# RetNet retention and SwiGLU: float32 Strassen products replaced by three 12-bit products each

## The chip, the cores and the metric

The kernel runs on one core of one Trainium2 chip. TensorE (PE in the profile) multiplies matrices into PSUM, whose eight banks hold 128 x 512 float32 values each; VectorE (DVE), ScalarE (ACT) and GpSimd (POOL) work element by element, GpSimd on SBUF alone; DMA queues move data between HBM and SBUF, and most are issued from SyncE (SP). The metric is the device time in microseconds of one execution; the median of three runs of the kernel before is 708.61 us (707.46 to 709.76).

## The reference

Retention over 4 sequences of 768 tokens with 8 heads of 64, and then a SwiGLU block on the 3072 tokens:

```python
for t in range(S):
    state = gamma[None, :, None, None] * state + np.einsum('bhd,bhe->bhde', k[:, :, t], v[:, :, t])
    y[:, :, t] = scale * np.einsum('bhd,bhde->bhe', q[:, :, t], state)
...
x = np.ascontiguousarray(attn_out.transpose(0, 2, 1, 3)).reshape(B * S, H * D)
g = x @ w_gate
silu = g * (1.0 / (1.0 + np.exp(-g)))
val = x @ w_val
return (silu * val @ w_out).astype(np.float32)
```

d_model is 512 and d_ff is 1536. q, k, v and the result are float32; the three weights come as 64-bit floats, and the kernel makes float32 of them from their two words.

## The kernel before

**Segments and stages.** Tokens are taken in four segments of 768: three chunks of 128 positions in each of two sequences. x^T lies in SBUF as `xT`, the hidden activations as `hT` (12 blocks of 128 of d_ff, each with the tokens of both sequences). For each segment there is an up stage (gate and value products, silu, multiply) and a down stage (the product with w_out), and beside the down stage of segment s runs the retention of segment s + 1, whose small matmuls are put between the big ones (`retention`, from L497, all through `mm` at L502). So the kernel goes: start, up 0, down 0 with retention 1, up 1, down 1 with retention 2, and so on to down 3.

**Up stage of segment 0** (`up`, L673): for each of 12 blocks f, one level of Strassen in Winograd's form. Two sequences by two halves of d_model meet gate and value by two halves of d_model, seven products instead of eight, each of two float32 matmuls of 384 columns (L679). Their sums lie in `ring` (weights) and `xs` (activations). Meanwhile the weights come in from HBM as 64-bit words, are turned into float32 on ScalarE, VectorE and GpSimd (`convert_a`, `convert_b`, `convert_c`), summed on VectorE (`sums_t`, L284) and written back to HBM for later segments (`keep_wt`). The string table `beside` says what goes beside which product.

**Up stages of segments 1 to 3** (`up2`, L749): a second level of Strassen. 21 units of seven products each (seven at the upper level for each of three groups of four blocks), each product two float32 matmuls of 192 columns (L790). Results are put together from PSUM by VectorE and ScalarE, and by additions of whole tiles on GpSimd (`stage`; its calls show up at L755 and L825). Units are loaded into a ring of six, and their sums are made once (`sums_u`, L159) and saved.

**Down stages** (`down`, L866): one level of Strassen over both sequences, both halves of d_ff and both halves of the output; for each of three chunks u seven products of six float32 matmuls of 256 columns (L873, L883). w_out is held in SBUF with its sums (`wot`, 12 x 7 x 256 floats per partition between six tiles), and four sums of hidden activations are made for each chunk (`sum_h`, L861).

**Order.** The schedule is written by hand. In `up2` each operation is an event at a time in units of matmuls, and the events are sorted; in `down`, `step` counts products and `DUE` says at which count a part of the retention is put in. An engine works through its instructions in the order in which they were issued, with semaphores for what it needs from others. SP's DMAs are likewise in order.

Of the kernel before, what the change touches and what calls it, by code (L numbers as in the profile page):

```python
# [10 lines left out]
F32 = mybir.dt.float32  # L11
I32 = mybir.dt.int32
# [4 lines left out]
P = 128  # L17
# [14 lines left out]
NQ = NF // 4  # L32
NU = 7 * NQ
RING = 6
# [4 lines left out]
NTAB = GDEC0 + NP  # L39


@with_exitstack
def tile_retnet_swiglu(
# [13 lines left out]

# [9 lines left out]
    def place(name, n):  # L90
        return consts.tile([P, n], F32, name=name)

    hsp, midp, loadp, iop = (place(nm, n) for nm, n in (
        ("hsp", 4 * FH * P), ("midp", 6 * TA), ("loadp", 8 * 512), ("iop", 6 * 512)))
    hT = consts.tile([P, NF, 2, TH], F32, name="hT")
    ring = [consts.tile([P, 7 * KH * P], F32, name=f"ring{i}") for i in range(RING)]
    banks = [psum.tile([P, 512], F32, name=f"bank{i}") for i in range(8)]
    turn = {}

    def bank(tag):  # L100


        own = {"s": (4, 5), "y": (6, 7)}[tag]
        turn[tag] = turn.get(tag, -1) + 1
        return banks[own[turn[tag] % len(own)]]


    chunks = {}

    def load_chunk(c, places):  # L110

        for t in places:
            own = chunks.setdefault(c, [])
            nc.sync.dma_start(out=t, in_=(k_t, q_t, v_n, k_n)[len(own)][c])
            own.append(t)

    def seg_chunks(s):

        p, pos = divmod(s * L, NCK)
        return [(2 * p + i) * NCK + pos + j for j in range(L) for i in range(2)]  # L120

    tab = consts.tile([P, NTAB], F32, name="tab")


    wt = {}
    wot = [consts.tile([P, 7, DH], F32, name=f"wot{j}") for j in range(FH)]
    T3, B22, B12, T1, B11, B21, T2, T4 = 0, 1, 2, 2, 3, 4, 5, 6


    U1, U11, U21, U3, U22, U2, U4 = range(7)  # L130
    unit_b = [kept.tile([P, 7, 2, 4, P], F32, name=f"unitb{q}", tag=f"unitb{q}")
              for q in range(NQ)]
    unit_t = [kept.tile([P, 2, 7, P], F32, name=f"unitt{n}", tag=f"unitt{n}")
              for n in range(NU)]
    PRODUCTS = (1, 5, 6, 2, 7, 3, 4)
    SLOT = {1: B11, 5: T1, 6: T2, 2: B21, 7: T3, 3: B22, 4: T4}
# [4 lines left out]
    def keep_wt(f):  # L141

        q, b, h = f // 4, f // 2 % 2, f % 2
        nc.sync.dma_start(out=unit_b[q][:, :, h, ds(2 * b, 2)],
                          in_=wt[f].rearrange("p a (k f) -> p a k f", k=KH))

    units = {}

    def load_unit(n, whole, slot=None):
        t = ring[n % RING if slot is None else slot]  # L150
        t = t.rearrange("p (h a b) -> p h a b", h=2, a=7)
        if whole:
            nc.sync.dma_start(out=t, in_=unit_t[n])
        else:
            nc.sync.dma_start(out=t[:, :, ds(U11, 4)],
                              in_=unit_b[n // 7][:, SLOT[PRODUCTS[n % 7]]])
        units[n] = t

    def sums_u(n, engine=nc.vector):  # L159

        w = units[n]
        sub = engine.tensor_tensor

        def first():
            sub(w[:, :, U1 : U3 + 1 : 3], w[:, :, ds(U3, 2)], w[:, :, U11 : U3 + 1 : 2],
                op=ALU.subtract)

        def last():
            sub(w[:, :, U4], w[:, :, U21], w[:, :, U2], op=ALU.subtract)  # L169
            nc.sync.dma_start(out=unit_t[n], in_=w)  # L170

        return [first,
                lambda: sub(w[:, :, U2], w[:, :, U22], w[:, :, U1], op=ALU.subtract),
                last]


# [3 lines left out]
    def span(piece):  # L180

        kind, a, h = piece
        if kind == "up":
            return wt[a], B22, 4
        return wot[a], (B22, B11)[h], 2

    def load_piece(piece):

        kind, a, h = piece
# [5 lines left out]
        else:  # L195
            top, low = (w_out[ts(a + FH * i, P)] for i in range(2))
            parts = ([(low[:, DH:], 0), (top[:, DH:], 1)],
                     [(top[:, :DH], 0), (low[:, :DH], 1)])[h]
        to, slot, n = span(piece)
        to = to[:, ds(slot, n)]  # L200
        if w_gate.dtype != F32:
# [4 lines left out]
        for src, i in parts:  # L206
            if w_gate.dtype != F32:
                src = src.bitcast(U32)
            if len(src.shape) == 3:
                c = src.shape[1]  # L210
                t = to[:, i:].rearrange("p a b -> p (a b)")[:, : c * src.shape[2]]
                t = t.rearrange("p (c f) -> p c f", c=c)
            else:
                t = to[:, i]
            nc.sync.dma_start(out=t, in_=src)

# [40 lines left out]

    def convert_c(piece, halves=1):
        if piece in raw:
            d, lo, hi = words_of(piece)
            n = d.shape[1] // halves
            for i in reversed(range(halves)):
                nc.gpsimd.tensor_tensor(d[:, ts(i, n)].bitcast(I32),
                                        d[:, ts(i, n)].bitcast(I32),  # L270
                                        lo[:, ts(i, n)].bitcast(I32), op=ALU.add)
            del raw[piece]

    def sums_t(piece, parts=range(3)):
        kind, a, h = piece
        w = span(piece)[0]
        sub = nc.vector.tensor_tensor
# [3 lines left out]
        for o, x, y in [((both, w[:, ds(B22, 2)], w[:, ds(B12, 2)])),  # L281
                          ((w[:, T2], w[:, B22], w[:, T1])),
                          ((w[:, T4], w[:, B21], w[:, T2]))][parts[0] : parts[-1] + 1]:
            sub(o, x, y, op=ALU.subtract)  # L284
        if kind == "up" and parts[-1] == 2:
            keep_wt(a)

    pieces = [("up", f, 0) for f in range(NF)] + [
        ("down", n % FH, 1 - n // FH) for n in range(2 * FH)]
    sign_banks = {0: (0, 1), 1: (4, 5)}

    def scale(what, engine):
        return lambda n: what(cs[n], engine)
# [35 lines left out]
    beside[11, 4] = "k4 k5"  # L334
    beside[8, 2] = "D D"

    def aside(f, place):
        if (f, place) == (8, 2):
            raw_places["down"][:0] = [hsp[:, ts(i, 1024)] for i in range(2)]
        do(beside.get((f, place), ""))  # L340

    to_load = {"up": [("up", f, 0) for f in range(NF)],
               "down": [("down", n % FH, 1 - n // FH) for n in range(2 * FH)]}
# [105 lines left out]

# [698 lines left out]
```

## Time and profile before

The profiled execution has a span of 706.6 us, 2.0 us below the median of the runs. The stages, from the chain of waits and the profile's windows (busy times in us):

| stage | from-to, us | length | TensorE | VectorE | ScalarE | GpSimd |
|---|---|---|---|---|---|---|
| start | 0-29.5 | 29.5 | 24.3 | 16.5 | 13.1 | 7.5 |
| up 0, first part | 29.5-69.1 | 39.6 | 36.8 | 32.5 | 28.6 | 12.1 |
| up 0, rest | 69.1-143.6 | 74.5 | 74.5 | 64.1 | 52.8 | 32.6 |
| down 0 + retention 1 | 143.6-216.5 | 72.9 | 71.3 | 56.5 | 16.1 | 13.0 |
| up 1 | 216.5-317.6 | 101.1 | 98.6 | 83.4 | 34.3 | 53.3 |
| down 1 + retention 2 | 317.6-386.7 | 69.1 | 69.1 | 36.5 | 16.6 | 11.9 |
| up 2 | 386.7-483.4 | 96.7 | 96.7 | 62.0 | 34.3 | 48.5 |
| down 2 + retention 3 | 483.4-552.6 | 69.2 | 69.1 | 35.1 | 16.1 | 12.8 |
| up 3 | 552.6-649.4 | 96.8 | 96.8 | 62.2 | 34.3 | 48.5 |
| down 3 | 649.4-701.7 | 52.3 | 52.2 | 17.3 | 5.0 | 0.0 |
| last copies and stores | 701.7-706.6 | 4.9 | 1.6 | 0.0 | 0.5 | 0.0 |

Busy time of TensorE is that of records whose ends are modelled and which overlap, so it says that there are few gaps, not how much of the array works. The page's first part gives the shares over the whole span and the number of instructions:

```profile
PE 691.0 (98%) x5132; PEld 601.3 (85%) x5132; DVE 466.0 (66%) x830; ACT 251.5 (36%) x514; POOL 240.2 (34%) x147
```

### The profile page before, as it was taken

How to read it: one execution, taken by the hardware profiler on the slowest of the kernel's cores; microseconds unless marked ns; L12 is line 12 of the kernel's file. 1: busy time of each engine (PE TensorE's matmuls, PEld its weight loads, DVE VectorE, ACT ScalarE, POOL GpSimd, SP SyncE). 2: the span in 40 equal slices, each digit the busy share in tenths (PEclk: the TensorE clock that was granted, in tenths of full speed). 3: DMA queues.
4: the chain of work that ended last, by engine and by line, in shares of the span. 5: the costliest groups of instructions: out<-in, count | busy, mean ns of one | idle time of the engine just before them, and what ended most of it. 6: DMA issues, size and time to landing. Idle time of an engine off the chain costs nothing.

```text
span 706.6 us, 12979 instructions
## 1 busy us (share of the span) xinstructions
PE 691.0 (98%) x5132; PEld 601.3 (85%) x5132; DVE 466.0 (66%) x830; ACT 251.5 (36%) x514; POOL 240.2 (34%) x147
## 2 busy tenths in 40 slices
PE   7998999999999899999999999999999999999998
PEld 7654555578888899998888999998888999999887
DVE  3887998778858987876353675657551666657420
ACT  2658777511333233421322333331222324342000
POOL 0334444403300738280230455474210182644000
PEclk9999999999999999999999999999999999999999
DMA  9798897657999858581570555562291255630010
GB/s 316 261 369 281 284 300 239 176 138 221 354 355 369 316 183 306 206 252 45 188 305 1 186 198 198 194 210 67 84 374 38 86 205 209 209 105 0 24 37 30
DMA packets 63356, 139.92 MB, mean 198 GB/s; under 512 B 6336, under 2 KB 30272, under 8 KB 63296
## 3 DMA queue, kind: packets, MB, share of 16 engines
q1 hardware_dynamic: 59552, 132.81, 55.6%
q10 hardware_dynamic: 3744, 6.29, 2.4%
q8 instruction: 40, 0.66, 0.4%
q14 instruction: 20, 0.16, 0.1%
HBM read 102.51 MB, written 36.57 MB: 197 GB/s over the span
## 4 chain that ended last, share of the span: by engine, by line
PE 83%; DMA 8%; DVE 3%; issue 3%; ACT 2%; POOL 1%; SPq 0%; DVEq 0%; ACTq 0%; POOLq 0%
PE bank L790 38%; PE bank L873 23%; PE bank L679 13%; PE bank L502 4%; PE bank L883 4%; DMA out_dram<-iop 1%; DMA unitt<-ring 1%; DMA loadp<-in_w_gate_dram 1%; DMA hsp<-in_w_gate_dram 1%; DMA hT<-in_v_n_dram 1%; DMA loadp<-in_q_t_dram 1%; DMA ring<-unitb 1%; DMA hT<-in_k_t_dram 1%; DVE ring L169 0%; DVE iop L755 0%
## 5 line engine op out<-in xcount | busy, mean ns | idle before, releaser
L790 PE MATMUL bank<-loadp,ring 128*128 128x192 f32 x720 | 140.6, 327 | 0.7 <-DVE iop L755 0.7
L873 PE MATMUL bank<-wot,hsp 128*128 128x256 f32 x576 | 129.4, 382 | 0.0
L790 PEld LDWEIGHTS bank<-loadp,ring 128*128 128x128 f32 x720 | 120.4, 190 | 2.4 <-DVE iop L755 1.3
L873 PEld LDWEIGHTS bank<-wot,hsp 128*128 128x128 f32 x576 | 108.1, 190 | 16.0 <-issue 1.4
L755 DVE TENSOR_TENSOR iop<-bank,iop 128x384 f32<-128x384 f32 x144 | 79.7, 556 | 50.1 <-PE bank L790 46.8
L790 PE MATMUL bank<-xs,ring 128*128 128x192 f32 x432 | 88.0, 326 | 1.2 <-DVE iop L755 1.2
L755 ACT COPY hsp<-bank 128x384 f32<-128x384 f32 x90 | 42.9, 478 | 102.5 <-PE bank L790 94.0
L825 POOL TENSOR_TENSOR hT<-iop 128x768 f32<-128x768 f32 x36 | 67.1, 1863 | 35.4 <-DVE iop L755 35.4
L755 POOL TENSOR_TENSOR iop<-hsp,midp 128x768 f32<-128x768 f32 x9 | 16.3, 1812 | 174.8 <-ACT hsp L755 140.3
L790 PEld LDWEIGHTS bank<-xs,ring 128*128 128x128 f32 x432 | 73.1, 190 | 1.5 <-DVE iop L755 1.5
L790 PE MATMUL bank<-xT,ring 128*128 128x192 f32 x324 | 66.3, 327 | 0.2 <-DVE midp L755 0.2
L873 PE MATMUL bank<-wot,hT 128*128 128x256 f32 (+1 forms) x300 | 65.9, 373 | 0.5 <-ACT iop L960 0.4
L679 PE MATMUL bank<-xs,ring 128*128 128x384 f32 x192 | 64.7, 488 | 1.1 <-ACT iop L700 0.5
L873 PEld LDWEIGHTS bank<-wot,hT 128*128 128x128 f32 x300 | 54.9, 190 | 8.4 <-DVE iop L948 0.6
L679 PEld LDWEIGHTS bank<-xs,ring 128*128 128x128 f32 x192 | 36.1, 190 | 27.8 <-ACT iop L700 1.1
L790 PE MATMUL bank<-hsp,ring 128*128 128x192 f32 x288 | 56.7, 326 | 0.5 <-ACT hsp L755 0.5
L790 PEld LDWEIGHTS bank<-xT,ring 128*128 128x128 f32 x324 | 54.7, 190 | 1.4 <-DVE iop L755 0.8
L755 DVE TENSOR_TENSOR midp<-bank,midp 128x384 f32<-128x384 f32 x72 | 39.9, 554 | 17.9 <-PE bank L790 14.8
L679 PE MATMUL bank<-xT,ring 128*128 128x384 f32 x144 | 49.8, 489 | 1.8 <-DVE hT L716 1.6
L790 PEld LDWEIGHTS bank<-hsp,ring 128*128 128x128 f32 x288 | 48.4, 190 | 0.8 <-ACT hsp L755 0.8
L944 DVE TENSOR_TENSOR iop<-bank,iop 128x256 f32<-128x256 f32 x12 | 5.1, 424 | 64.7 <-PE bank L873 51.8
L679 PEld LDWEIGHTS bank<-xT,ring 128*128 128x128 f32 x144 | 26.9, 190 | 21.9 <-DVE hT L716 2.2
(152 smaller groups left out, 973.4 us busy)
## 6 DMA issues: line engine op xcount, KB each, us to landing
ring<-unitt SPq DMA_DIRECT2D x50, 896.0 KB, 4.6
unitt<-ring SPq DMA_DIRECT2D x21, 896.0 KB, 6.0
unitb<-ring SPq DMA_DIRECT2D x12, 896.0 KB, 7.0
ring<-unitb SPq DMA_DIRECT2D x21, 512.0 KB, 5.9
out_dram<-iop ACTq DMA_DIRECT2D x23, 256.0 KB, 2.5
loadp<-in_w_val_dram SPq DMA_DIRECT2D x18, 256.0 KB, 4.1
loadp<-in_w_gate_dram SPq DMA_DIRECT2D x9, 512.0 KB, 6.6
midp<-in_w_out_dram SPq DMA_DIRECT2D x12, 256.0 KB, 6.0
```

What stands on the lines that cost most here:

```text
L502: nc.tensor.matmul(o, a, b, start=start, stop=True, skip_group_check=True)
L679: nc.tensor.matmul(o, w[:, slot, k], a[:, k], start=(start and k == 0), stop=(stop and k == KH - 1), skip_group_check=True)
L755: events.append((t, len(events), lambda: fn(*args, **kw)))
L790: nc.tensor.matmul(o[:, h], w[:, h, slot], rhs, start=(start and h == 0), stop=True, skip_group_check=True)
L825: by_block(9.5, 13.5, lambda r: pool(to[:, r], u2[:, r], p5[:, r], op=add))
L873: nc.tensor.matmul(o[:, cols], a[:, k], wot[k][:, slot, cols], start=(start and k == 0), stop=(k == FH - 1), skip_group_check=True)
L883: nc.tensor.matmul(o, a_dn(0, 0, u)[:, k], wot[k][:, B11], start=(k == 0), stop=(k == FH - 1), skip_group_check=True)
L944: tt(ev[0][:, DH:], wb, u2, op=ALU.add)
```

## The change

Up 0 stays as it was. In the rest, four things change.

**Three 12-bit products.** A float32 operand is split into a high part of 12 bits and a rest, in tiles of type float32r (`R12`) with three planes, such that the three plane-wise products, added up in one PSUM bank, make the product up to a factor. The one operand is split by `near_*` (plane 0 on ScalarE, plane 1 on VectorE from two SBUF tiles, plane 2 on GpSimd as their sum), the other by `far_*` (plane 0 on ScalarE, plane 1 on GpSimd, plane 2 on VectorE from two SBUF tiles, and a scaling of it on ScalarE). Each float32 matmul becomes three float32r matmuls.

**Up stages 1 to 3** (`up3`): one level of Strassen instead of two. For each block f there are seven products of three planes by two halves, of 384 columns; the weights, with their sums, are loaded from HBM as in up 0's order (`w_up`) and split anew in every segment, in groups of 768, 768 and 256 columns (`weights`). The activations' seven operands are split once for a segment, in the down stage before it (`make_x`).

**Down stages:** no Strassen. For each block f and each of six groups of 128 tokens, three matmuls of 512 columns into one of banks 0 to 5, which gather all 12 blocks. The hidden activations of a block are split just ahead (`h_split`); w_out is no longer held but streamed: in down 0 read as float32 and split, with the planes written to HBM (`w_dn3`), in later ones read as planes.

**Retention** uses banks 6 and 7 alone: scores, mixing in two parts with a small read between them (`fence`), and states take turns in them, each at its own half step (`PARTS`).

Everything after the start is an event with a planned time; all events are sorted by it. The planned times set only the order on each engine.

```diff
+CUT = 1.0 + 2.0 ** -13
+FAR = 4096.0
+ONE = 4095.0
...
+    def near_a(o, x):
+        act(o[0], x, AF.Copy, scale=CUT / FAR)
+
+    def near_b(o, x):
+        stt(o[1], f32(o[0]), -FAR, x, op0=mul, op1=add)
+
+    def near_c(o):
+        pool(o[2], f32(o[0]), f32(o[1]), op=add)
+
+    def far_a(o, x):
+        act(o[0], x, AF.Copy, scale=CUT)
+
+    def far_b(o, x):
+        pool(o[1], f32(o[0]), x, op=sub)
+
+    def far_c(o):
+        stt(o[2], f32(o[0]), 1.0 / FAR, f32(o[1]), op0=mul, op1=sub)
+
+    def far_d(o):
+        act(o[2], f32(o[2]), AF.Copy, scale=FAR / ONE)
...
+    def make_x(t, s, p):
+        for m in range(4):
+            at(t + 0.4 * m, sum_x, m)
+        for k, n in enumerate((1, 2, 0)):
+            b = t + 0.3 + 0.6 * k
+            at(b, lambda n=n: far_a(*x_part(s, p, n)))
+            at(b + 0.8, lambda n=n: far_b(*x_part(s, p, n)))
+            at(b + 2.2, lambda n=n: far_c(x_part(s, p, n)[0]))
+            at(b + 3.0, lambda n=n: far_d(x_part(s, p, n)[0]))
...
+    ORDER = (1, 2, 6, 5, 7, 3, 4)
+    GROUPS = [(3, 3), (0, 3), (6, 1)]
+    PASS_U, PASS_D = 0.1768, 0.232
+    PROD = 6 * PASS_U
+    UPT = 7 * PROD
...
+        at(t - 7.2, begin)
+        at(t - 5.6, lambda: near_b(*it["o"]))
+        at(t - 4.4, lambda: near_c(it["o"][0]))
+
+    def product(s, f, p, o, start):
+        slot = SLOT[p]
+        g = 2 if slot == 6 else 0 if slot >= 3 else 1
+        w = ups[f, g].rearrange("p a (n k f) -> p a n k f", k=KH, f=P)[:, :, slot - GROUPS[g][0]]
+        for a in range(3):
+            for k in range(KH):
+                nc.tensor.matmul(o, w[:, a, k], xs_of[s][:, a, OP[p], k],
+                                 start=start and a == k == 0, stop=a == 2 and k == KH - 1,
+                                 skip_group_check=True)
+
+    def up3(s, f, t):
+        x, z, wb = (banks[i][:, :TH] for i in (6 + f % 2, 0, 1))
...
+        for g, first in enumerate((0, 3, 6)):
+            weights(t + first * PROD, f, g)
+        for n, p in enumerate(ORDER):
+            o = {1: x, 6: x, 7: x, 4: x, 2: z, 5: wb, 3: wb}[p]
+            at(t + n * PROD, product, s, f, p, o, p in (1, 2, 5))
+        e = lambda n: t + (n + 1) * PROD + 0.1
+        at(e(0), copy, p1, x)
+        at(e(1), tt, c11, z, p1, op=add)
+        at(e(1) + 0.7, act, c11, c11, AF.Silu, scale=ONE)
+        at(e(2), copy, u2, x)
+        at(e(3), copy, p5, wb)
+        at(e(4), tt, hT[:, f, 1], x, p5, op=add)
+        at(e(5), tt, hT[:, f, 0], wb, u2, op=add)
+        at(e(5) + 0.7, tt, hT[:, f, 0], hT[:, f, 0], c11, op=mul)
+        at(e(6), act, x, x, AF.Silu, scale=ONE)
+        at(e(6) + 0.7, tt, hT[:, f, 1], hT[:, f, 1], x, op=mul)
...
+        at(t - 7.5, begin)
+        at(t - 6.3, lambda: near_b(it["o"], hT[:, f].rearrange("p i t -> p (i t)")))
+        at(t - 5.2, lambda: near_c(it["o"]))
...
+        at(t - 13.0, lambda: nc.sync.dma_start(out=raw_w, in_=w_dn[f]))
+        at(t - 7.3, begin)
+        at(t - 6.5, lambda: far_b([wo[f][:, i] for i in range(3)], raw_w))
+        at(t - 4.5, lambda: far_c([wo[f][:, i] for i in range(3)]))
+        at(t - 3.5, lambda: far_d([wo[f][:, i] for i in range(3)]))
+        at(t - 2.0, lambda: nc.sync.dma_start(out=w_dn3[f], in_=wo[f].bitcast(U32)))
+
+    def down(f, tok):
+        i, u = divmod(tok, L)
+        for a in range(3):
+            nc.tensor.matmul(banks[tok], hs[f][:, a, ds(i * TH + u * P, P)], wo[f][:, a],
+                             start=f == a == 0, stop=f == NF - 1 and a == 2,
+                             skip_group_check=True)
...
+    PARTS = {1: [("s", 0, 0)], 2: [("s", 0, 1)], 4: [("m", 0, 0)], 5: [("o", 0, 0)],
+             6: [("t", 0, 0)], 7: [("s", 1, 0)], 8: [("s", 1, 1)], 10: [("m", 1, 0)],
+             11: [("o", 1, 0)], 12: [("t", 1, 0)], 13: [("s", 2, 0)], 14: [("s", 2, 1)],
+             16: [("m", 2, 0)], 17: [("o", 2, 0)], 18: [("t", 2, 0)]}
```

The scores' decay (`decayed`, VectorE), the scalings of q and k (`scale_q2`, `scale_k2`, GpSimd), the eight copies of y from PSUM (`bring_y`, ScalarE) and the states' sums (`keep_state`) do what they did in `retention`. The staging buffers of up 0 (`loadp`, `hsp`, `midp` and the rest) share their space with the planes of the later stages.

## The prediction, written before the changed kernel was run

> **What bounds the kernel now.** I read the chain of waits first, then the stretches between the stages, then single lines of VectorE and GpSimd. The chain of waits, its shares by engine and then its pieces (start, length, what; x counts instructions), gives the bound and the price of a product:
>
> ```profile
> PE 83%; DMA 8%; DVE 3%; issue 3%; ACT 2%; POOL 1%; SPq 0%; DVEq 0%; ACTq 0%; POOLq 0%
> ```
>
> ```profile
> 69.14 72.48 PE bank L679 x224
> ...
> 386.66 95.09 PE bank L790 x584
> ...
> 653.67 31.08 PE bank L873 x144
> ```
>
> TensorE is 83% of the chain. A float32 product leaves two records, so a record costs 72.48/224 = 323.6 ns at 384 columns, 95.09/584 = 162.8 at 192 and 31.08/144 = 215.8 at 256: two passes of N/2.4 ns and 2.5 to 3.6 more. The windows by stage (us, busy time with instructions, clock, DMA share):
>
> ```profile
> 69.10:143.60 74.50, 74.50 (x233) 44.19 (x233) 64.06 (x121) 52.81 (x94) 32.63 (x21) 1.00 0.80 249
> 143.60:216.50 72.90, 71.30 (x825) 60.54 (x824) 56.46 (x103) 16.10 (x45) 12.97 (x10) 1.00 0.81 276
> 216.50:317.60 101.10, 98.58 (x594) 96.14 (x593) 83.42 (x151) 34.29 (x66) 53.27 (x29) 1.00 0.78 268
> 317.60:386.70 69.10, 69.10 (x795) 59.74 (x794) 36.47 (x60) 16.55 (x46) 11.85 (x9) 1.00 0.38 138
> 386.70:483.40 96.70, 96.70 (x593) 96.13 (x592) 62.03 (x115) 34.30 (x66) 48.53 (x27) 1.00 0.54 184
> 483.40:552.60 69.20, 69.07 (x794) 59.54 (x793) 35.14 (x59) 16.07 (x44) 12.84 (x10) 1.00 0.39 138
> 552.60:649.40 96.80, 96.80 (x594) 96.21 (x593) 62.15 (x115) 34.28 (x66) 48.49 (x27) 1.00 0.43 149
> 649.40:701.70 52.30, 52.23 (x248) 45.96 (x246) 17.28 (x25) 4.97 (x13) 0.00 (x0) 1.00 0.06 24
> ```
>
> The reader is to see: segment 0's up products end at 143.6 us, then down and up stages alternate, TensorE has almost no gap, and in a down stage GpSimd (last busy column) works only 12 to 13 us. The change will fill that column. What this may cost is in the next lines: durations (min/median/max, ns) of VectorE operations with both inputs in SBUF, and one stretch of GpSimd beside VectorE.
>
> ```profile
> L254 DVE TENSOR_SCALAR ring<-ring x12: 685/686/2905, 23.4 to 116.6; 128x1024 f32<-128x1024 f32 x12
> L169 DVE TENSOR_TENSOR ring<-ring x21: 409/424/1491, 169.7 to 301.8; 128x256 f32<-128x256 f32 x21
> L861 DVE TENSOR_TENSOR hsp<-hsp,hT x12: 951/958/1908, 153.5 to 678.4; 128x768 f32<-128x768 f32 x12
> L755 DVE TENSOR_TENSOR iop<-bank,iop x144: 541/558/558, 224.3 to 649.6; 128x384 f32<-128x384 f32 x144
> ```
>
> ```profile
> 300.65 1.99 POOL L755 TENSOR_TENSOR midp<-hsp,midp 128x768 f32<-128x768 f32 x1
> ```
>
> ```profile
> 301.82 1.10 DVE L169 TENSOR_TENSOR ring<-ring 128x256 f32<-128x256 f32 x1
> 302.85 0.54 DVE L755 TENSOR_TENSOR midp<-bank,midp 128x384 f32<-128x384 f32 x1
> ```
>
> L169 usually takes 424 ns; here it starts at 301.82, GpSimd ends at 302.64, and L169 ends at 302.92, 0.28 us later, which is its data time. It waited for the whole GpSimd operation. L755 of VectorE, with one input in PSUM, never passes 558 ns. So a two-SBUF-input operation and a GpSimd operation exclude each other.
>
> **What the Trainium skill says.** "SBUF — State Buffer", section Who interferes with whom: the pair of ports shared by VectorE and GpSimd is an exclusive lock, held for a whole instruction, and a VectorE instruction with two SBUF inputs contends with a GpSimd one that reads SBUF. The trace agrees (424 to 1491 ns). "FP8 and Floating Point Precision", TensorE Precision Notes: full float32 is four passes, a reduced float32 is read and cut to 22 bits. The four passes agree with the records; no run so far shows a reduced product. "TensorE: Matmul & The Clock Gate", Back-to-back issue gap: N/2.4 + 2.5 ns warm; the trace's 215.8 and 162.8 agree.
>
> **The change, part by part.**
>
> *Up stages 1 to 3.* Removed: 294 float32 products of 192 columns, 588 x 164.4 = 96.7 us, and 4.4 us of waits in the first (101.1). Added: 12 x 7 x 6 = 504 float32r products of 384 columns. If one is a single pass it takes 160 + 2.5 = 162.5 ns, 6.83 us for a step f, 81.9 us for a stage. Weights fit: the old stage loads a 128x128 tile every 162.8 ns already. The bounds are this and the schedule's own constant, 0.1768 us, 7.43 a step.
>
> But each step must also split 1792 weight columns: on ScalarE 2 x 0.845 + about 0.40; on VectorE three operations of 768, 768 and 256 with two SBUF inputs; on GpSimd three additions. GpSimd takes 1.81 for 768 (L755 1.812) and, from 1.27 at 512 (L572 median 1.276) and that slope, 0.73 for 256: 4.35 us. VectorE holds the lock N/0.96 ns, 0.80 + 0.80 + 0.27, and 0.40 for the one multiply of two SBUF tiles: 2.27. Lock time is 6.6 of 6.83 us, before anything waits. So I walk the queues through one step from the end of GpSimd's second 768 addition, in the order of instructions of the changed kernel, with dependent starts 0.06 to 0.08 after an end, and an independent VectorE or ScalarE operation starting 0.07 to 0.09 before the last ends, as in the timeline of before:
>
> - VectorE multiply (waiting for the lock) to 0.42; its 256 split to 0.75
> - GpSimd 256 addition 0.83 to 1.56
> - VectorE split of the first 768, locked until then, to 2.38
> - behind it in VectorE's queue the c11 addition (558 ns, L755), to 2.84
> - ScalarE silu (0.49) to 3.39, copy u2 to 3.80, next 768 first part (0.845) to 4.58
> - VectorE split of it, 0.95, to 5.59; GpSimd's addition, 1.81, to 7.48, where the loop closes.
>
> The loop takes 7.48 us without TensorE in it; TensorE's own is 6.83 to 7.43. A stage is then 12 x 7.48 = 89.8, three 269.4 against 294.6: -25.2.
>
> *Down stage 3 (no retention).* 216 products of 512 columns: 215.8 ns each (46.6 us) to the schedule's 0.232 (50.1); I take 48.4. The lock needs (1.81 + 0.82) x 12 = 32, hidden. Against 52.3: -3.9.
>
> *Down stages 1 and 2.* TensorE: 48.4 + 14.65 (retention's products, L502 in the stretch 317.6 to 386.7) = 63. Lock: 12 hidden-activation splits, 12 x (1.81 + 0.82) = 31.6; ten scalings (L572 1.27, L578 1.04), 11.5; x split on GpSimd, per pair 512, 256 and 1024 columns, 1.27 + 0.73 + 2.40 (L269, 2410 ns for 1024) = 4.4, three times 13.2; on VectorE its second half 1.87 and its sums 1.13, three times 9. Sum 65. Two steps' splits (4) lie before the stage, handing over adds about 2 and the last step's products 4. In the retention part, three steps of TensorE take 17 us and of the lock 20. ScalarE's eight copies of y (L622, 366 ns) delay the state products behind them. I take 70 each, against 69.1 and 69.2: +1.7. Bounds: 64 (lock hidden) and 78.
>
> *Down stage 0.* The same, and w_out is split here: 12 x (GpSimd 1.27 + VectorE 0.55) = 22 more. Lock 87; less 6 before the stage, plus 2 for handing over and 4 at the end: 87. Before: 72.9, with the sums and saves that now go. +14.1. Bounds 66 and 98.
>
> *Start, up stage 0, end.* Until 143.6 the work stays; two state products move in, and the first splits come beside a VectorE that is 86% busy: +1.0 (bounds 0 and 4). w_out's writes queue on SP behind conversions that the next load waits for anyway. Tail 4.7 (was 4.9): a copy of 0.69 and the store's 2.5 remain. DMA falls in up stages to 0.9 MB per 7.5 us, and is no bound.
>
> Sum: 143.6 + 1.0 + 87 + 269.4 + 140 + 48.4 + 4.7 = 694.1 against the span 706.6, -12.5. The median is 708.61, 2.0 above the span; so 696.1, I say 696. GpSimd's durations when it writes float32r, and VectorE's three-operand form with two SBUF inputs, are not in the trace: I take the float32 rows, since the element count is the same; below them would be only a missing lock, above perhaps 10% on GpSimd.
>
> **The rivals.**
>
> *TensorE paces everything.* If the three-operand form does not take the lock, or queues slip past each other: up 86 a stage (between 81.9 and 89.1), down 68, 66, 66, 48.4. Sum 144.6 + 68 + 258 + 132 + 48.4 + 4.7 = 655.7, with 2.0 about 658. For it: only 2.3 of 6.8 us a step are locked on VectorE. Against: 2905 ns at L254.
>
> *Queue waits behind the lock, slower than before.* One mechanism in the up step: the splits arrive just after a GpSimd addition began, wait 1.8 us instead of what the walk gives them (0.4 and nothing), and the additions behind them in VectorE's queue release c11's and x's banks late, so TensorE stops. With 0.9 us a step it is 36 x 0.9 = 33 more, 729. It decides from 12.5/36 = 0.35 us a step. For it: VectorE's queue is strictly in order here, and L755's results stand behind the splits. Against: GpSimd has 3 us a step free.
>
> *Reduced products take two passes.* Then 322.5 ns for 384: 13.5 us a step, 3 x 72.7 = 218 more in up stages, and 430 ns for 512, down stages at least 92.9 and 107.6: 138 more. About 1052. The records exclude nothing, the skill speaks against it.
>
> **How the numbers follow.** Own forecast 0.44 (682 to 710), TensorE pacing 0.20, queue waits 0.33, two passes 0.03. Range 655 to 735: it leaves out the two-pass case, the upper third of the queue waits and the lowest of the TensorE case. A measurement tells 0.3% (2.1 us) from no change. Faster: 0.34 + 0.20 = 0.54; same 0.04 + 0.02 = 0.06; slower 0.06 + 0.31 + 0.03 = 0.40.
>
> **What would show it.** Right: float32r products spaced 162 to 177 ns; in up stages about 90 us with VectorE's 768 splits often 1 to 2 us long; a first down stage longer than the others by some 17 us, with GpSimd at over 70%; a last one near 48. Wrong: splits that always take 0.95 us, up stages at 82 or over 97, or products spaced over 200.

## The result, and the profile after

The changed kernel takes 755.7 us (median of 4 runs, 754.1 to 757.5) against 708.0 (705.8 to 709.8): a ratio of 1.067 (95% interval 1.063 to 1.070), slower by about 48 us. Its profiled execution has a span of 753.8 us. From its page, busy time by engine (part 1), the TensorE clock in 40 slices (part 2) and the chain that ended last (part 4):

```profile
PE 686.9 (91%) x4724; PEld 563.6 (75%) x4724; DVE 479.3 (64%) x695; ACT 360.7 (48%) x693; POOL 405.7 (54%) x261
...
PEclk9999999989889999999898999999988999999999
...
PE 65%; POOL 8%; DVE 7%; issue 6%; DMA 6%; ACT 5%; SPq 2%; ACTq 0%; DVEq 0%; POOLq 0%
```

TensorE's share of the chain fell from 83% to 65%. GpSimd, VectorE and ScalarE now stand in it with 20%, and there are slices in which the clock was below full; before, every window had 1.00. The windows by stage (stretch, length, busy time of PE, PEld, DVE, ACT and POOL with instructions, granted clock, DMA share, GB/s):

```profile
64.00:144.60 80.60, 78.94 (x268) 46.44 (x269) 72.16 (x133) 59.60 (x105) 38.02 (x23) 0.99 0.82 273
144.60:249.80 105.20, 81.38 (x769) 61.73 (x768) 64.63 (x70) 45.20 (x88) 68.47 (x42) 0.88 0.61 202
249.80:344.40 94.60, 91.77 (x507) 88.17 (x506) 65.13 (x98) 48.30 (x97) 53.62 (x37) 0.98 0.42 147
344.40:428.70 84.30, 72.91 (x756) 56.39 (x755) 43.48 (x56) 32.62 (x66) 49.60 (x31) 0.92 0.50 173
428.70:521.80 93.10, 91.27 (x511) 87.00 (x510) 66.26 (x98) 47.84 (x97) 53.74 (x38) 1.00 0.44 150
521.80:606.50 84.70, 72.64 (x753) 56.29 (x752) 44.28 (x56) 31.94 (x64) 50.01 (x31) 0.90 0.51 173
606.50:699.70 93.20, 92.47 (x515) 87.81 (x514) 65.99 (x98) 48.00 (x97) 54.85 (x37) 1.00 0.36 120
699.70:747.00 47.30, 47.30 (x211) 39.14 (x210) 12.75 (x13) 9.32 (x12) 19.15 (x11) 1.00 0.50 168
```

The up stages (249.8, 428.7, 606.5) gained 3.6 to 6.5 us each on the ones before, and down 3 gained 5. The loss is in the three down stages that run beside retention: 105.2, 84.3 and 84.7 us for 72.9, 69.1 and 69.2. No engine is full there. TensorE has 11 to 24 us of gaps, and a granted clock of 0.88 to 0.92.

What a gap looks like is seen in down 1. From the timeline (start, length, engine, line, operation; in brackets the idle time before it and what released it):

```profile
363.21 1.54 POOL L654 TENSOR_TENSOR x<-x,chunk_x 128x512 fp32r<-128x512 f32 x1 [7.11 <-ACT x L651]
363.52 1.52 DVE L687 TENSOR_TENSOR tmp<-tmp,chunk_x 128x256 f32<-128x256 f32 x1
364.71 2.01 POOL L648 TENSOR_TENSOR gitem<-gitem 128x768 fp32r<-128x768 f32 x1
364.96 2.05 DVE L687 TENSOR_TENSOR tmp<-chunk_x 128x256 f32<-128x256 f32 x1
...
365.74 2.33 PE L810 MATMUL bank<-oitem,gitem 128*128 128x512 f32 x9
...
369.05 2.35 POOL L654 TENSOR_TENSOR x<-x,tmp 128x1024 fp32r<-128x1024 f32 x1 [1.45 <-ACT x L651]
...
371.43 1.22 DVE L657 SCALAR_TENSOR_TENSOR x<-x 128x1024 fp32r<-128x1024 f32 x1 [2.61 <-POOL x L654]
372.57 1.01 DVE L465 TENSOR_TENSOR tmp<-bank,tab 128x384 f32<-128x384 f32 x2
...
373.17 2.02 PE L446 MATMUL bank<-loads 64*64 64x128 f32 x32 [5.09 <-DVE tmp L465]
375.12 5.75 PE L810 MATMUL bank<-oitem,gitem 128*128 128x512 f32 x18
```

Read it from the bottom. TensorE is through with its products at 368.07 and waits for L465 (`decayed`), which frees the two banks for the next scores. L465 takes 0.5 us, and the products that it reads were done by 365.8. But in VectorE's queue it stands behind L657, the last part of the split of x (`far_c`), which waits for GpSimd's subtraction L654 (2.35 us). That one waits for ScalarE, and that for VectorE's sums L687, two of which took 1.5 and 2.05 us in place of 0.42: each ends 0.29 us after a GpSimd operation (364.75 and 366.72), as L169 did in the prediction's lines (0.28), so they were locked out. And when TensorE starts again, 18 products take 5.75 us; without a gap before them they take 4.4 (see the first experiment).

The same stands at 187.97 and 216.48 (gaps of 6.1 and 6.0 us), 399.55, 551.22 and 577.34 (4.4 each): the second and third pair of chunks in each of three down stages. I summed each stage from the trace's records, from its first product to the first of the next stage, so that lengths differ by 1 to 2 us from the windows. Part of the time at half clock lies in the gaps, so only TensorE's busy time at half clock is halved:

| down stage | length | TensorE idle | at half clock | of that TensorE busy | length - idle - half of the busy part |
|---|---|---|---|---|---|
| 0 | 103.7 | 23.8 | 23.9 | 19.1 | 70.3 |
| 1 | 85.5 | 11.4 | 13.7 | 10.8 | 68.7 |
| 2 | 87.0 | 12.1 | 17.1 | 13.4 | 68.2 |
| 3 | 49.2 | 0.0 | 0.0 | 0.0 | 49.2 |

The last column is an estimate of what TensorE needs at full speed. For down 1 and 2 it is about the whole length of these stages in the kernel before (69.1 and 69.2). So against the kernel before the loss is gaps (11 to 24 us) and the half clock after them (5 to 10 us), not the products. Against the prediction's sum, which had 63 us for TensorE in down 1 and 2, some 5 us are products as well.

### The profile page after: what moved, and what is told of

The parts are those of the page before. It is cut to its first block, busy times and chain, and to the rows that moved or that the text cites. A ratio compares the mean times of both kernels' runs of the same rounds, so it can differ in the third digit from the quotient of the medians.

```text
span 753.8 us, 12380 instructions
## 1 busy us (share of the span) xinstructions
PE 686.9 (91%) x4724; PEld 563.6 (75%) x4724; DVE 479.3 (64%) x695; ACT 360.7 (48%) x693; POOL 405.7 (54%) x261
## 4 chain that ended last, share of the span: by engine, by line
PE 65%; POOL 8%; DVE 7%; issue 6%; DMA 6%; ACT 5%; SPq 2%; ACTq 0%; DVEq 0%; POOLq 0%
PE bank L745 35%; PE bank L810 15%; PE bank L585 11%; PE bank L446 4%; DVE x L657 3%; POOL gitem L648 3%; POOL x L654 2%; ACT chunk_x L680 1%; POOL loads L518 1%; ACT gitem L642 1%; DMA rawp<-in_w_gate_dram 1%; DMA chunk_x<-wdn 1%; DMA hT<-in_q_t_dram 1%; DVE gitem L645 1%; DVE tmp L687 1%
## 5 line engine op out<-in xcount | busy, mean ns | idle before, releaser
L648 POOL TENSOR_TENSOR gitem<-gitem 128x768 fp32r<-128x768 f32 x120 | 226.3, 1886 | 140.3 <-DVE gitem L645 139.3
L745 PE MATMUL bank<-x,gitem 128*128 128x384 f32 x1296 | 238.6, 341 | 5.4 <-ACT tmp L118 5.4
L810 PE MATMUL bank<-oitem,gitem 128*128 128x512 f32 x864 | 225.6, 417 | 13.4 <-DVE hT L601 5.7
L745 PEld LDWEIGHTS bank<-x,gitem 128*128 128x128 f32 x1296 | 224.2, 189 | 14.5 <-ACT tmp L118 7.5
L810 PEld LDWEIGHTS bank<-oitem,gitem 128*128 128x128 f32 x864 | 168.8, 200 | 55.4 <-issue 8.2
L645 DVE SCALAR_TENSOR_TENSOR gitem<-gitem,loads 128x768 fp32r<-128x768 f32 x72 | 79.5, 1104 | 66.2 <-ACT gitem L642 66.2
L585 PE MATMUL bank<-first 128*128 128x384 f32 x336 | 112.5, 495 | 3.2 <-DVE hT L620 1.6
L585 PEld LDWEIGHTS bank<-first 128*128 128x128 f32 x336 | 64.0, 193 | 50.4 <-issue 2.3
L645 DVE SCALAR_TENSOR_TENSOR gitem<-gitem,hT 128x768 fp32r<-128x768 f32 x48 | 55.7, 1162 | 33.5 <-ACT gitem L642 33.5
L642 ACT ACTIVATE gitem<-loads 128x768 fp32r<-128x768 f32 x72 | 60.4, 843 | 3.0 <-DVE oitem L645 3.0
L118 ACT ACTIVATE bank<-bank 128x384 f32<-128x384 f32 x36 | 17.1, 475 | 76.5 <-PE bank L745 76.5
L657 DVE SCALAR_TENSOR_TENSOR x<-x 128x512 fp32r<-128x512 f32 (+2 forms) x27 | 42.7, 1607 | 8.5 <-POOL x L654 8.5
```

The lines of the kernel that those rows point to most:

```text
L118: events.append((t, len(events), lambda: fn(*args, **kw)))
L585: nc.tensor.matmul(o, w[:, slot, k], a[:, k], start=(start and k == 0), stop=(stop and k == KH - 1), skip_group_check=True)
L642: act(o[0], x, AF.Copy, scale=CUT / FAR)
L645: stt(o[1], f32(o[0]), -FAR, x, op0=mul, op1=add)
L648: pool(o[2], f32(o[0]), f32(o[1]), op=add)
L657: stt(o[2], f32(o[0]), 1.0 / FAR, f32(o[1]), op0=mul, op1=sub)
```

## The experiments

Theories: (A) *order*: `decayed` stands behind the split of x in VectorE's queue, and moving that split is enough. (B) *GpSimd and its lock*: GpSimd's operations are long, VectorE is locked out meanwhile, and whatever stands first in the queues is late. (C) *clock*: TensorE at half speed after gaps is itself a large part. (D) *late loads*: w_out's blocks come late in down 0.

### Moving the last parts of x's split, and the reads of w_out

```diff
-            at(b + 2.2, lambda n=n: far_c(x_part(s, p, n)[0]))
-            at(b + 3.0, lambda n=n: far_d(x_part(s, p, n)[0]))
+            at(b + 7.4, lambda n=n: far_c(x_part(s, p, n)[0]))
+            at(b + 8.2, lambda n=n: far_d(x_part(s, p, n)[0]))
```

> Only the order changes: in make_x the last two operations of x's split (far_c on VectorE, far_d on ScalarE) are put 5.2 planned us later, behind the decays of the next pair's scores. Queue theory (the decays, which release banks 6 and 7, stand behind far_c, which waits for far_b on GpSimd): the idle stretches of TensorE of 5 to 6 us before the second and third pair's scores go, and with them the half clock after them; down 0 from 105 to about 90, down 1 and 2 from 84 to about 70, total about 710. Port theory (VectorE's two-input operations and GpSimd together have too much to do in a down stage): the order is no matter, down 0 stays at 100 or more, down 1 and 2 at 80 or more, total above 740.

Measured: 760.1 us (ratio 1.073, 1.069 to 1.077). TensorE's timeline in down 1, at the place of the gap:

```profile
371.40 1.36 PE L446 MATMUL bank<-loads 64*64 64x128 f32 x32 [0.34 <-DVE tmp L465]
372.69 4.39 PE L810 MATMUL bank<-oitem,gitem 128*128 128x512 f32 x18
378.98 0.43 PE L446 MATMUL bank<-loads,states 64*64 64x128 f32 x2 [1.90 <-POOL loads L518]
380.38 0.55 PE L446 MATMUL bank<-loads,states 64*64 64x128 f32 x11 [0.97 <-POOL loads L518]
```

The gap before the scores is gone (0.34 us for 5.09) and the 18 products run at full speed (4.39). Down 1 and 2 are 80.1 and 81.3 for 85.5 and 87.0; down 0 stays at 104.2. But 2.9 us of gaps come back seven us later, at GpSimd's scaling of q (L518). And the three up stages are 97 to 99 us for 91 to 94: the third pair's split now reaches into them, and the first step's copies stand behind it. So the wait was named rightly, and moving it alone pays nothing: the queue theory's 710 is missed by 50.

```diff
-        at(t - 13.0, lambda: nc.sync.dma_start(out=raw_w, in_=w_dn[f]))
+        at(t - (13.0 if f > 1 else 26.0), lambda: nc.sync.dma_start(out=raw_w, in_=w_dn[f]))
```

> Only the loads of w_out's first two blocks as float32 are issued 13 planned us earlier. Theory: the silus of up 0's last block stand on ScalarE behind the first part of block 1's split, which waits 7 us for that load; TensorE's gap of 5.7 us at 151 goes and part of the half clock behind it: 6 to 9 us less, about 747. Rival: GpSimd and VectorE are what down 0 waits for, so that the gap comes back later: at most 2 us less.

Measured: 757.4 us in its one run; down 0 is 106.5 with 25.9 idle. The gap of 5.67 us at its start went, and one of 7.8 came at 164.9: GpSimd's queue waits there for the third block, whose read stands in SP's queue behind the write of block 0's planes. With both edits:

> The first two edits together. Queue theory: what they give adds up, about 702. Port theory: 740 or more.

Measured: 761.0 us in its one run; no better than the first alone. The 702 of gains that add is missed by 59.

The split late for the first two pairs only, so that the third is ready for the up stage:

```diff
+            late = 5.2 if p < 2 else 0.0
+            at(b + late + 2.2, lambda n=n: far_c(x_part(s, p, n)[0]))
+            at(b + late + 3.0, lambda n=n: far_d(x_part(s, p, n)[0]))
```

> The third and fourth parts of the split of x go 5.2 us later for the first two pairs only; the third pair keeps its place, so that x is whole before the up stage. Theory 'the scores wait stands in VectorE's queue behind that split': down stages 1 and 2 at 80 to 81 us (84.3, 84.7 in the changed kernel), up stages unchanged at 93 to 95: about 745 us. Rival 'VectorE and GpSimd have too much work in the stage, the order is no matter': 752 us or more.

Measured: 749.5 us (1.058, 1.052 to 1.065), down 1 and 2 at 81.5 and 83.4. That is 6 us less than the changed kernel, between the two figures. Theory A is true of the gaps of 4 to 6 us and explains about an eighth of the loss.

### Leaving out one addition on GpSimd

```diff
-        at(t - 4.4, lambda: near_c(it["o"][0]))
...
-                nc.tensor.matmul(o, w[:, a, k], xs_of[s][:, a, OP[p], k],
+                nc.tensor.matmul(o, w[:, min(a, 1), k], xs_of[s][:, a, OP[p], k],
...
-        at(t - 5.2, lambda: near_c(it["o"]))
```

and the same index in `down`.

> Leaves out the third plane of the near split (the addition on GpSimd); TensorE reads plane 1 twice in its place and does as much as before. It takes 253 us of GpSimd away, and what they hold of the port. Port theory: down 0 to about 75, down 1 and 2 to 66, up stages from 93 to 89, total about 675. Queue theory: x's split still runs over GpSimd and VectorE ahead of the decays, so the gaps before the second and third pair's scores stay at 3 us or more; down 1 and 2 at 76 or more, down 0 at 90 or more, total about 725.

Measured: 732.1 us in its one run. Down 0, 1 and 2 are 96.3, 79.2 and 78.0. Half of the loss goes when GpSimd has 253 us less to do, the order of the queues being the same; 24 us remain. The port theory's 675 is missed by 57, and the result lies near the queue theory's 725: the gaps before the second and third pair's scores shrink, but stay at 2.7 to 4.3 us. So neither GpSimd's load nor the order is the whole cause by itself. In the up stages a step takes 7.30 us here, in all three; in the changed kernel 7.50.

### Idle products in the gap

```diff
                 if what == "s":
+                    if p and g:
+                        at(t, fill, banks[5], 6)
                     at(t, scores_of, p, g)
```

> Six idle products (zeros times the decay table, 384 columns of float32, 0.65 us each, 3.9 us in all, added into a bank where they change nothing) stand in TensorE's queue right before the second scores group of the second and third pair in down stages 0, 1 and 2, where the changed kernel has gaps of 4.4 to 6.1 us and then runs at half clock. Nothing else waits less. Theory 'an idle TensorE loses half its clock': the half-clock time falls from 23.9, 13.7 and 17.1 us to about 10, 0 and 3.4, half of that is saved, 17 to 20 us: 736 to 739 us. Rival 'the clock falls for another reason (load, time)': half-clock time as before, 754 to 758 us. Third 'VectorE and GpSimd pace the stage': the clock comes back but the gaps grow by as much, 750 us or more.

Measured: 752.2 us (1.062, 1.059 to 1.065). The windows around the same gap, the changed kernel first (columns as above; the clock is the third figure from the end):

```profile
366.00:368.10 2.10, 2.08 (x9) 1.36 (x8) 2.10 (x3) 0.18 (x1) 1.60 (x2) 1.00 0.87 314
368.10:373.10 5.00, 0.00 (x0) 0.00 (x0) 2.39 (x5) 2.84 (x5) 2.35 (x1) 0.82 0.29 114
373.10:376.50 3.40, 3.33 (x35) 2.81 (x36) 2.62 (x6) 1.38 (x2) 1.90 (x2) 0.50 0.13 9
376.50:379.90 3.40, 3.40 (x13) 2.72 (x12) 0.73 (x1) 0.00 (x0) 3.40 (x3) 0.76 0.90 342
```

and with the idle products:

```profile
366.00:368.10 2.10, 2.10 (x13) 1.75 (x10) 2.10 (x3) 0.00 (x0) 1.81 (x2) 1.00 0.97 352
368.10:372.10 4.00, 4.00 (x13) 2.09 (x11) 1.38 (x3) 2.62 (x4) 2.36 (x1) 1.00 0.34 134
372.10:373.40 1.30, 0.06 (x1) 0.00 (x0) 1.30 (x3) 0.49 (x1) 0.00 (x0) 1.00 0.00 0
373.40:376.50 3.10, 3.06 (x40) 2.45 (x41) 2.98 (x5) 1.30 (x2) 1.68 (x1) 1.00 0.20 50
```

The clock stays at 1.00: the half-clock time of down 1 and 2 goes from 13.7 and 17.1 us to nothing, that of down 0 from 23.9 to 13.7. So gaps in TensorE's work are what halves it. But the time falls by only 3.6 us. Down 1 and 2 are 2.6 and 3.7 us shorter, together 6.3, where the half clock had cost 12 by the table above; the rest of the run is longer by the difference. The scores start at 373.40 with the idle products and at 373.17 without: VectorE's queue comes to L465 when it does, whatever TensorE's speed. Idle products counted (about 7.8 us a stage), TensorE's gaps in each of these stages are 1 us longer than without them. So (C) is a consequence of the gaps, with a price of its own of some 6 of the 31 us that down 1 and 2 lose against the kernel before.

### Taking the splits off GpSimd

The activation's third plane and x's second one are made by VectorE in the down stages:

```diff
-        at(t - 5.2, lambda: near_c(it["o"]))
+        at(t - 5.2, lambda: tt(it["o"][2], f32(it["o"][0]), f32(it["o"][1]), op=add))
...
-            at(b + 0.8, lambda n=n: far_b(*x_part(s, p, n)))
+            at(b + 0.8, lambda n=n: far_bv(*x_part(s, p, n)))
```

where `far_bv` is `far_b` with VectorE's `tt`.

> In the down stages the third part of the hidden activation's split (12 of 768 columns a stage) and the second part of x's split go from GpSimd to VectorE, so that about 35 us of GpSimd's work and of its lock become about 18 us of VectorE's own. Theory 'GpSimd's length and its lock make the queues late': 730 to 742 us, VectorE's 768 splits in the down stages back at 0.95 us. Rival 'VectorE's one queue is the limit, whatever is in front': the stages get longer by a part of the added 18 us, 756 to 775 us.

Measured: 727.8 us (1.028, 1.025 to 1.031), 28 us less. The groups by line of the changed kernel (busy us, mean ns after the bar), and then of this one:

```profile
L648 POOL TENSOR_TENSOR gitem<-gitem 128x768 fp32r<-128x768 f32 x120 | 226.3, 1886 | 140.3 <-DVE gitem L645 139.3 <-PE bank L810 1.0
L645 DVE SCALAR_TENSOR_TENSOR gitem<-gitem,hT 128x768 fp32r<-128x768 f32 x48 | 55.7, 1162 | 33.5 <-ACT gitem L642 33.5
L657 DVE SCALAR_TENSOR_TENSOR x<-x 128x256 fp32r<-128x256 f32 x9 | 16.6, 1843 | 3.1 <-POOL x L654 3.1
L657 DVE SCALAR_TENSOR_TENSOR x<-x 128x512 fp32r<-128x512 f32 x9 | 14.8, 1644 | 2.8 <-POOL x L654 2.8
```

```profile
L787 DVE TENSOR_TENSOR gitem<-gitem 128x768 fp32r<-128x768 f32 x48 | 48.9, 1019 | 0.7
L645 DVE SCALAR_TENSOR_TENSOR gitem<-gitem,hT 128x768 fp32r<-128x768 f32 x48 | 48.8, 1017 | 22.8 <-ACT gitem L642 22.8
L660 DVE SCALAR_TENSOR_TENSOR x<-x 128x512 fp32r<-128x512 f32 x9 | 6.2, 687 | 0.0
L660 DVE SCALAR_TENSOR_TENSOR x<-x 128x256 fp32r<-128x256 f32 x9 | 3.8, 421 | 0.0
```

An addition of 768 columns costs 1.02 us on VectorE and 1.89 on GpSimd, and the last part of x's split falls from 1.84 to 0.42 (256 columns) and from 1.64 to 0.69 (512): what was above these figures was waiting, as behind the lock. VectorE got 71 us of new work (48.9, and 22.3 for x), and yet the down stages fell to 91.8, 75.9 and 75.8. Theory B is shown, by more than its own figures said, and its rival, that VectorE's queue is the limit whatever is in front, is refuted. What isn't separated is B's two halves: the edit takes away both GpSimd's longer operations in the chain and the times in which they lock VectorE out.

> The two edits before together (late split for two pairs, splits on VectorE) and the stores of the output issued by SyncE in place of ScalarE, whose queue holds the first copy of the up stage behind them. If the three causes are separate the gains add: 722 to 732 us, up stages at 90. If one of them is the whole cause: no faster than the better of the two alone.

Its third edit, in `finish`: `nc.sync.dma_start` in place of `nc.scalar.dma_start`. Measured: 723.7 us (1.022, 1.019 to 1.025). That is 32 us less than the changed kernel, where the first two edits alone add to 34. The gains nearly add, as the first of the two theories has it, though the third edit was never run alone. The up stages are at 91.9, 91.0 and 91.5 (93.3, 93.8 and 94.2 with the splits on VectorE alone). Down 0 is 95.3, 3.5 us longer than with the splits on VectorE alone, and keeps 18.3 us of gaps.

### Down stage 0

Two kernels on top of the last one move its reads and splits of w_out earlier, the second one x's split later too. In both, block 3 of w_out is read into block 1's place ahead of block 1's split, so that block 1's products take block 3's values.

```diff
+        e = 0.0 if f == 1 else 2.2
+        at(t - (20.0 if f > 1 else 26.0), lambda: nc.sync.dma_start(out=raw_w, in_=w_dn[f]))
+        at(t - e - 7.3, begin)
...
-                    make_x(t + 3.0, nxt, p)
+                    make_x(t + (4.7 if p < 2 else 3.0), nxt, p)
```

> The kernel with all three edits (f4_all_three), and in down stage 0 the reads of w_out's blocks are issued 7 to 13 us earlier and their splits (but for block 1's) 2.2 us earlier. Theory 'down stage 0 is long because its first blocks come late through SyncE's queue and ScalarE waits for them ahead of the last gates': down stage 0 at 82 to 87 us (95.3 in f4_all_three), the gap before the second block's products (3.65 us) and the one before block 9's (3.91 us) gone: 711 to 716 us. Rival 'the same waits stand elsewhere in the stage, since VectorE has 69 us of work there': 720 us or more.

> As g1_dn0_early, and the split of x starts 1.7 us later for the first two pairs, so that the state's update stands ahead of it in VectorE's queue; the scores of the next pair wait for that update (gaps of 1.5 to 3.1 us before them in f4_all_three). Theory 'order in VectorE's queue': the gaps go, 1.9 us in each of five places and some half clock, 6 to 10 us less than g1_dn0_early: 703 to 709 us. Rival: the split of x then delays the next decayed scores by as much, within 2 us of g1_dn0_early.

Measured: 721.6 and 730.6 us. The first lies in its rival's range, but doesn't tell the theories apart, since that order makes a wait of its own, as this line of its timeline shows:

```profile
158.66 0.63 ACT L651 ACTIVATE oitem<-chunk_x 128x512 fp32r<-128x512 f32 x1 [17.17 <-DMA chunk_x<-wdn]
```

ScalarE waits 17 us for the later block, and the last gates stand behind it. The second is slower than the first in all three stages (100.4, 75.8, 77.1 us for 93.6, 74.4, 73.6): the gaps before the scores are then at `decayed` again, as its rival said, and cost more than it said.

So I took the splits off the path of that stage instead: down 0 multiplies the unsplit activation by the unsplit block in float32, and w_out's split is only stored for later.

```diff
+        if s == 0:
+            nc.tensor.matmul(banks[tok], hT[:, f, i, ts(u, P)], raws[f], start=f == 0,
+                             stop=f == NF - 1, skip_group_check=True)
+            return
```

> The kernel with all three edits (f4_all_three), and down stage 0 multiplies the unsplit activation by the unsplit w_out block in float32, as the kernel before did for that stage without its level of Strassen: 72 products of 0.86 us for 216 of 0.227. No split of the activation there; w_out is still split and stored for the later stages, but no product of that stage waits for it. TensorE's sum is 62 + 14.7 = 77 us. Theory 'the splits in the queues ahead of TensorE cost down stage 0 its time': 79 to 84 us (95.3 in f4_all_three), 708 to 713 us in all. Rival 'the chain of retention and of x's split paces that stage': 88 us or more, 716 us or more.

Measured: 707.3 us (20 runs, 705.7 to 709.4), ratio 0.9981 (0.9967 to 0.9995). The windows of down 0, up 1 and most of down 1:

```profile
144.60:223.40 78.80, 78.71 (x687) 39.31 (x686) 37.74 (x65) 35.55 (x74) 28.18 (x20) 1.00 0.72 234
223.40:318.00 94.60, 91.45 (x490) 86.42 (x489) 67.27 (x98) 48.79 (x99) 56.73 (x39) 0.96 0.48 168
318.00:392.00 74.00, 69.60 (x772) 54.67 (x771) 52.21 (x78) 33.68 (x68) 14.66 (x9) 1.00 0.59 204
```

TensorE is busy for 78.7 of 78.8 us at full clock, with 13 us more of products than in the split form, and the stage (144.5 to 225.8, first product to the next stage's first) takes 81 us for 95. So the splits ahead of TensorE, and what they wait for, were what made that stage long; its rival, the chain of retention and x's split, is refuted, since that chain is still there. Whether the splits waited more for GpSimd and the lock or for w_out's reads (D), it doesn't tell: the reads of w_out changed too, earlier and into other buffers. This kernel is the fastest of all, by 6.4% against the changed one. Against the one before it is 0.2% faster, less than the 0.3% that the prediction called no change.

> As h1_dn0_plain, with the second part of x's split back on GpSimd (only the activation's split stays off it). If VectorE's queue length ahead of the state's update is what makes the gaps of 1.5 to 3.1 us before the next pair's scores, they shrink and the stages 1 and 2 go from 74.4 and 75.2 to 71 to 73: 3 to 6 us less than h1_dn0_plain. If GpSimd's slower subtraction and its lock count more: 2 to 6 us more than h1_dn0_plain.

Measured: 717.6 us (1.013, 1.009 to 1.017), 10 us more. Three subtractions a pair back on GpSimd (1.03, 1.43 and 2.43 us where VectorE takes 0.42, 0.69 and 1.22) lengthen down 1 and 2 by 3.3 and 3.5 us and up 0 with down 0 by 2.1. GpSimd is busy for 39% and 41% of down 1 and 2 in this run; so it is the length of its operations within a chain, or the lock, that counts, and not how full it is.

## Why the prediction was wrong

Its forecast was 696 us, faster. By its own steps, with the windows above:

| step | predicted | measured | difference |
|---|---|---|---|
| start and up 0 | 144.6 | 144.6 | 0.0 |
| down 0 | 87 | 105.2 | +18.2 |
| up 1 to 3 | 269.4 | 280.9 | +11.5 |
| down 1 and 2 | 140 | 169.0 | +29.0 |
| down 3 | 48.4 | 47.3 | -1.1 |
| tail | 4.7 | 6.8 | +2.1 |
| span | 694.1 | 753.8 | +59.7 |

**Where it failed: down stages 0 to 2, 47 of the 60 us.** The step "Down stages 1 and 2" takes TensorE's time (63) and the lock's (65) as overlapping, and puts a little over the larger, 70, with 78 as its worst. Measured are 84.3 and 84.7. The overlap is what it had wrong: TensorE stands idle for 11.4 and 12.1 us in them. The sum would be right where each engine has other work while it waits. In-order queues don't give that: VectorE's queue has the split of x ahead of `decayed`, the split waits for GpSimd, GpSimd for ScalarE, ScalarE for VectorE, and TensorE for `decayed`. In a chain the times add. For the up step I had walked the queues one by one; for the down stage, where the order of retention is in the queues too, I only added up. The step "Down stage 0" is built in the same way, and fell short by 18; it foresaw that this would be the longest of the three, by 17; measured 21.

**TensorE's own 63 was too small as well.** It is about 68: in the fastest kernel, down 1 runs at full clock and takes 72.8 us with 4.4 idle. The 216 products take 49.2 (down 3, 48.4 in the sum). The rest, 19, stands beside retention's products, for which the sum had 14.65, their time in the kernel before. Why they cost more here is not shown.

**A right mechanism in the wrong place.** The rival "queue waits behind the lock, slower than before" is what happened, but it was put into the up step, at 0.9 us a step, and gave 729. Up steps lose 0.2 us to it, see below. In the down stages 0 to 2, where no rival put it, TensorE's gaps sum to 47 us. Since the range's upper end of 735 was drawn from that place, the time was out of it.

**The up stages' 89.8.** The walk through the queues gave 7.48 us a step; in the steady part it is 7.50 in all three stages. TensorE's own step, 6.83 to 7.43 in the prediction, is 7.30 (without the addition on GpSimd; 42 products at a median spacing of 174 ns are 7.31). So that addition costs 0.2 us a step, not 0.9. That 7.48 and 7.50 agree is not luck, for the loop is there piece by piece. The prediction's walk starts at the end of GpSimd's second addition of 768 columns, here at 476.99:

```profile
475.15 1.84 POOL L648 TENSOR_TENSOR gitem<-gitem 128x768 fp32r<-128x768 f32 x1 [1.29 <-DVE gitem L645]
...
476.38 1.03 DVE L118 TENSOR_TENSOR hT<-hT,tmp 128x384 f32<-128x384 f32 x1
...
477.33 0.41 DVE L645 SCALAR_TENSOR_TENSOR oitem<-oitem,loads 128x256 fp32r<-128x256 f32 x1
...
477.83 0.74 POOL L648 TENSOR_TENSOR oitem<-oitem 128x256 fp32r<-128x256 f32 x1 [0.84 <-DVE oitem L645]
...
478.15 1.23 DVE L645 SCALAR_TENSOR_TENSOR gitem<-gitem,loads 128x768 fp32r<-128x768 f32 x1
...
480.67 0.85 ACT L642 ACTIVATE gitem<-loads 128x768 fp32r<-128x768 f32 x1
...
481.55 0.96 DVE L645 SCALAR_TENSOR_TENSOR gitem<-gitem,loads 128x768 fp32r<-128x768 f32 x1 [1.70 <-ACT gitem L642]
...
482.65 1.85 POOL L648 TENSOR_TENSOR gitem<-gitem 128x768 fp32r<-128x768 f32 x1 [1.29 <-DVE gitem L645]
```

The ends, counted from there, are 0.42, 0.75, 1.58, 2.39, 4.53, 5.52 and 7.51; the walk had 0.42, 0.75, 1.56, 2.38, 4.58, 5.59 and 7.48. The 0.80 us for which it lets a split of 768 columns hold the lock follows from the slope between the medians of its lines L169 and L861, (958 - 424)/512 = 1.04 ns a column. (Its line L254 is no operation with two SBUF inputs, TENSOR_SCALAR reads one tile; the walk doesn't use it.) The splits of 768 columns, with minimum, median and maximum in ns:

```profile
L645 DVE SCALAR_TENSOR_TENSOR gitem<-gitem,loads x72: 957/959/2216, 246.9 to 689.4; 128x768 fp32r<-128x768 f32 x72
```

In the steady part every second one takes 1.20 to 1.25 us, the wait of the walk; the longest stand beside the end of a down stage. What is over 90 us in an up stage is at its start: from a stage's first product to the next stage's it is 94.2, 92.0 and 90.9. In the first step the first copy stands on ScalarE behind the stores of the output and the first groups' splits (gaps of 2.8, 1.8 and 0.7 us), and in up 1 a stretch at half clock follows. The windows count up to 2 us of the down stage's last products too. In the kernel with all three edits, with the stores on SyncE, the stages are within 2 us of 90; in the fastest kernel up 1 is at 96.0 again, with a gap of 3.15 us in the first step and the half clock after it.

**The half clock.** No term of the sum had it. It stands in 55 us of the three down stages and costs about 22 of them by the table above; by the idle products' run about half of its price in down 1 and 2 comes back as long as the queues are as they are.

**Right:** one pass for a float32r product (174 ns at 384 columns, 228 at 512, inside the bounds taken, though not at their lower ends), the up step with its loop, down 3, the start, and the lock itself. "GpSimd at over 70%" in down 0 was 65% (68.5 of 105.2).

**What stays open.** The span of the fastest kernel here (705.2) is 11 us over the sum's 694.1. Its three up stages take 278.3 for 269.4 and its down 1 and 2 take 148.0 for 140, while its down 0 takes 81.3 for 87. Also open: how the loss divides between the length of GpSimd's operations and the lock; and how much of down 0's length in the split form was late reads (D), which neither the earlier reads of the first two blocks nor the order with block 3 ahead showed.

## What to carry to other kernels

Where several engines take turns at one small chain, and each has an in-order queue, the stage's time is not the fullest engine's: write down for each instruction that frees a bank what stands ahead of it in its queue, and walk that. An engine that is half idle can still be too slow: ask for the length of its operation in the chain, and for whom it locks out, before giving it work. And a repair that moves one wait should be judged by the next stage too.

## What the runs showed of the hardware

- After gaps TensorE's granted clock was 0.5, in stretches of 3.41 us and its multiples (6.83, four times 10.24), whose starts lie on a grid of that step in each trace. The Trainium skill, "TensorE: Matmul & The Clock Gate", section What's actually happening, has a free-running window of 3413 ns and half rate after an idle one; the traces agree on the window, but it need not be idle throughout. Cut on that grid, the thirteen traces of the changed kernel and its variants have 2605 windows at full rate. All 90 in which TensorE was busy for less than 43%, by its records, were followed by one at half rate, none of the 2462 with more than 57%, and 18 of the 53 between. So a gap of 1.9 us was enough where it fell into one window (377.67 to 379.55 in the kernel with all three edits; the window from 377.08 is busy for 1.53 of 3.41 us, and the next one is at half rate), and one of 3.1 us passed where it fell into two (175.53 to 178.60 with the splits on VectorE alone: busy for 1.50 and 2.25 us, and no half rate after it).
- A GpSimd operation writing float32r took as long as one in float32: 1.84 us (median) for 768 columns, where the kernel before showed means of 1.81 to 1.87. VectorE's form with a scalar and two SBUF inputs waits for it just as the plain one: 0.96 us at 768 columns (median), up to 2.52.
